# First blocks of the mixture of experts in plain fp32 for four experts, without split parts, and the table of places by one VectorE pass

## The chip, the cores and the metric

The kernel runs on one core of a Trainium2 chip. The metric is the device time of one execution in microseconds (us), lower is better. The times shown are a median of three runs; the profile is of one further execution.

## The reference

A windowed attention (8 batches, 8 heads, 576 tokens, head size 64, window 128) is followed by a mixture of experts with two experts chosen per token:

```python
scores = scale * q @ k^T + bias, masked to 0 <= i - j < 128
attn = softmax(scores); x = (attn @ v) as [4608, 512]
logits = x @ w_gate; noisy = logits + log1p(exp(x @ w_noise)) * noise
top2 = the two largest of noisy; top2_w = softmax over the two
for e in range(8):
    h = maximum(x[mask] @ w1[e], 0.0)          # 512 -> 1024
    out[mask] += top2_w * (h @ w2[e])          # 1024 -> 512
```

## The kernel before

The program is straight-line code whose order is made while it is built: strands of work (generators) yield operations with an engine, an estimated cost and a rank, a small planner (class Order) takes for each free engine the ready operation of lowest rank, and so writes every engine's queue. On the chip each queue runs in that order; a row whose input is late holds all rows behind it on its engine.

There are two phases. In the first, 96 attention units (4 pairs of heads times 3 groups of query blocks for each of 8 batches) are computed in fp32: scores (L455, L448), maxima and bias on VectorE (L473), exponentials on ScalarE (L480), transposes (L492) and the product with v (L523). When a batch is done, its rows are transposed and stored (L632, L635), and `route` computes the gates, ranks the tokens of each expert by a small matmul (L723 to L727), and builds two tables: `which_line` (L759) and `which_place` (L765, ten instructions of 64 columns per batch), whose product on TensorE (L770) lists token numbers per expert. GpSimd scatters that list to memory (L843). Batch b + 1 is routed only when batch b is.

After two batches, NF = 5 experts each have at least FIRST = 256 listed tokens (places are padded up to that), and TensorE fills gaps of the attention with these first blocks: 5 blocks of 256 tokens, each in 8 steps of 128 hidden units. A step is an up product into one PSUM bank (`ups`, `mm1`, L1086), a relu (`middle`, L1108 or L1110), and a down product into two banks (`downs`, `mm2`, L1136). Operands are split into a high and a low part in fp32r, and each product is three matmuls (high by high, low by high, high by low). The parts cost other engines work: a weight tile is cast (ScalarE or VectorE) and subtracted (L962, GpSimd or VectorE), the tokens too (L1079), and the hidden units (L1125, VectorE).

In the second phase all other tokens are computed with f16 parts, three matmuls per product as well. Each expert has room for 1216 tokens: an expert with a first block has 960 left, in blocks of 512 and 448; the others have blocks of 512, 384 and 320 (`BLOCKS`). The last block of each expert but the last one is computed turned round (`mm2_flipped`, L1141). Tiles of the first phase end in a (axh, w1ha, ahh), those of the second begin with b or end in b (bxh, w1hb, bhh). The second phase can begin when batch 7 is listed and its tokens are gathered (L1034), scaled, turned and split.

The lines that name the sizes and the splits:

```python
CUTS = (2,)
FIRST = (256,)
NF = 5
BLOCKS = (((256, 512), (768, 448)), ((0, 512), (512, 384), (896, 320)))
second.extend(Block(e, s0, c, NPAD, rings2) for e in range(E) for s0, c in BLOCKS[e >= NF])
```

## Time and profile before

| what | value |
|---|---|
| median of 3 runs | 1215.79 us (1214.66 to 1219.39) |
| profiled execution | 1212.61 us |
| its span, first to last instruction | 1210.7 us |
| PE (TensorE) busy | 1142.3 us, 94% of the span |
| DVE (VectorE) busy | 775.9 us, 64% |
| ACT (ScalarE) busy | 547.3 us, 45% |
| POOL (GpSimd) busy | 310.7 us, 26% |
| mean granted TensorE clock | 0.988 of full |

Busy shares are means over stages that differ: the attention, a short stage in which the rest of the first blocks and the routing of the last batches are left, and the second phase. A matmul's duration in the trace holds its time through the array as well, so that TensorE can be counted busy while it starts nothing new; how dense it is worked is read from the starts of its instructions.

### The profile page before, as it was taken

The numbers are of one execution on the slowest core, as the hardware profiler recorded it, in microseconds if no ns is written. First come the engines' busy times: TensorE is split into PE (matmuls) and PEld (weight loads), VectorE is DVE, ScalarE is ACT, GpSimd is POOL, SyncE is SP. The second block draws the span as 40 slices with busy tenths as digits, with TensorE's granted clock in tenths as the row PEclk, the third lists the DMA queues.
The fourth block names the chain that finished last, engine by engine and source line by source line (L and its number), as shares of the span: only waits on it lengthen the run. The fifth ranks groups of instructions, "written<-read, shape, count | busy, mean of one in ns | idle before, by whom it ended". The sixth has DMA issues, their size and how long they took to land.

```text
span 1210.7 us, 20898 instructions
## 1 busy us (share of the span) xinstructions
PE 1142.3 (94%) x7336; PEld 690.1 (57%) x7336; DVE 775.9 (64%) x2483; ACT 547.3 (45%) x1378; POOL 310.7 (26%) x343
## 2 busy tenths in 40 slices
PE   7998899999997889999999999999999999999995
PEld 4666677777776764554544544545545654575552
DVE  6798787788898897664664674584563473373310
ACT  8776666667633353441432433342432441252311
POOL 5000121231255661320330331233033320332211
PEclk9999999999999999999999999999999999999998
DMA  8896545553267597562761862663663391352221
GB/s 289 281 319 208 172 130 172 161 151 125 77 184 179 125 280 217 134 186 91 178 187 45 206 171 54 186 191 58 193 166 62 80 264 41 62 114 45 35 27 23
DMA packets 138987, 177.57 MB, mean 147 GB/s; under 512 B 25728, under 2 KB 89472, under 8 KB 138880
## 3 DMA queue, kind: packets, MB, share of 16 engines
q1 hardware_dynamic: 120960, 135.87, 35.3%
q0 software_dynamic: 17920, 40.33, 17.5%
q8 instruction: 59, 0.97, 0.3%
q14 instruction: 48, 0.39, 0.1%
HBM read 134.76 MB, written 41.40 MB: 146 GB/s over the span
## 4 chain that ended last, share of the span: by engine, by line
PE 58%; DVE 13%; DMA 8%; issue 4%; POOL 1%; ACT 0%; SPq 0%; POOLq 0%; another core or an unknown queue 0%; DVEq 0%
PE bank L1086 23%; PE bank L1136 16%; PE bank L1141 8%; DMA mraw<-in_w_dram 5%; PE bank L523 2%; PE bank L492 2%; DMA xg<-xs_dram,ix 2%; DVE wam L988 2%; PE bank L1066 2%; PE bank L455 2%; DVE hot L765 1%; POOL out_dram L1215 1%; DVE bxl L1076 1%; DVE fit L1051 1%; DMA raw<-in_w_dram 1%
## 5 line engine op out<-in xcount | busy, mean ns | idle before, releaser
L1125 DVE SCALAR_TENSOR_TENSOR bhl<-bank,bhh 128x512 f16<-128x512 f32 (+3 forms) x152 | 93.9, 618 | 282.9 <-ACT bhh L1108 282.7
L1215 POOL DMA_INDIRECT out_dram<-yo,ix x70 | 110.3, 1575 | 534.3 <-ACT yo L245 480.4
L1108 ACT ACTIVATE bhh<-bank 128x512 f16<-128x512 f32 (+3 forms) x143 | 77.7, 543 | 332.8 <-PE bank L1086 331.9
L1086 PE MATMUL bank<-bxh,w1hb 128*128 128x512 f16 (+3 forms) x608 | 213.5, 351 | 0.0
L1086 PE MATMUL bank<-bxl,w1hb 128*128 128x512 f16 (+3 forms) x608 | 213.4, 351 | 0.0
L1086 PE MATMUL bank<-bxh,w1lb 128*128 128x512 f16 (+3 forms) x608 | 213.4, 351 | 0.0
L1086 PEld LDWEIGHTS <-w1hb 128*128 128x128 f16 x1216 | 118.0, 98 | 104.8 <-issue 1.9
L480 ACT ACTIVATE p<-p,nm 128x256 f32<-128x256 f32 (+2 forms) x288 | 133.8, 469 | 8.5 <-DVE nm L473 8.4
L1136 PE MATMUL bank<-w2hb,bhl 128*128 128x512 f16 (+1 forms) x352 | 133.5, 379 | 4.2 <-DVE bhl L1125 4.2
L1136 PE MATMUL bank<-w2hb,bhh 128*128 128x512 f16 (+1 forms) x352 | 133.7, 380 | 0.6 <-ACT bhh L1108 0.5
L1136 PE MATMUL bank<-w2lb,bhh 128*128 128x512 f16 (+1 forms) x352 | 133.4, 379 | 0.0
L1136 PEld LDWEIGHTS <-bhh 128*128 128x128 f16 (+1 forms) x704 | 67.3, 98 | 72.9 <-issue 4.6
L473 DVE CUSTOM_DVE_ANT_0 p<-bank,bias 128x256 f32<-128x256 f32 (+2 forms) x288 | 95.5, 380 | 17.4 <-PE bank L455 15.8
L1086 PEld LDWEIGHTS <-w1lb 128*128 128x128 f16 x608 | 59.5, 98 | 54.7
L962 POOL TENSOR_TENSOR w1la<-raw,w1ha 128x512 fp32r<-128x512 f32 x35 | 48.7, 1392 | 161.9 <-ACT w1ha L245 115.2
L523 PE MATMUL bank<-pT,vraw 128*64 128x128 f32 (+3 forms) x896 | 81.2, 303 | 5.6 <-ACT p L480 3.3
L492 PE MATMUL bank<-ident,p 128*128 128x128 f32 x512 | 83.2, 287 | 1.6 <-DVE pT L249 0.7
L1034 POOL DMA_INDIRECT xg<-xs_dram,ix x70 | 70.0, 1000 | 43.0 <-issue 37.9
L988 DVE TENSOR_REDUCE wam<-mraw 128x1 f32<-128x1024 f32 x56 | 67.7, 1211 | 19.9 <-DMA mraw<-in_w_dram 19.6
L455 PE MATMUL bank<-qk 64*128 64x256 f32 (+1 forms) x512 | 70.7, 389 | 10.2 <-DVE nm L473 5.3
L1141 PE MATMUL bank<-bhl,w2hb 128*128 128x448 f16 (+1 forms) x224 | 75.5, 337 | 0.0
L1141 PE MATMUL bank<-bhh,w2lb 128*128 128x448 f16 (+1 forms) x224 | 75.5, 337 | 0.0
(219 smaller groups left out, 2119.9 us busy)
## 6 DMA issues: line engine op xcount, KB each, us to landing
raw<-in_w_dram SPq DMA_DIRECT2D x208, 256.0 KB, 3.9
mraw<-in_w_dram SPq DMA_DIRECT2D x56, 512.0 KB, 6.6
qk<-in_qk_dram SPq DMA_DIRECT2D x32, 608.0 KB, 4.5
out_dram<-xg SPq DMA_DIRECT2D x10, 1024.0 KB, 8.6
vraw<-in_v_dram SPq DMA_DIRECT2D x16, 512.0 KB, 3.9
xs_dram<-x SPq DMA_DIRECT2D x32, 256.0 KB, 3.4
vraw<-in_v_dram SPq DMA_DIRECT2D x16, 128.0 KB, 5.5
xg<-xs_dram,ix POOLq DMA_INDIRECT x70, 4.8
```

The lines of the kernel that those rows point to most:

```text
L455: nc.tensor.matmul(s[h][:, o:o + c], qk[half, i * 128:i * 128 + 128], qk[half, QW + k0:QW + k0 + c], start=True, stop=True)
L473: nc.vector.tensor_tensor_reduce(out=p[:, z, h, 0:c], in0=s[h][:, o:o + c], in1=bv, scale=-0.125, scalar=3.0e38, op0=OP.add, op1=OP.min, a ...
L480: nc.scalar.activation(pv, pv, AF.Exp, bias=nm[:, z, h:h + 1], scale=-1.0, accum_out=den[:, z, 2 * g + h:2 * g + h + 1])
L492: nc.tensor.transpose(t[:, z], p[:, h, a:a + 128], ident)
L523: nc.tensor.matmul(o[half, o0:o0 + c], t[p0:128, kb, hh:hh + D], w, start=m == 0, stop=m == len(lst) - 1)
L988: yield dve(1.13, rank, lambda: nc.vector.tensor_reduce(o, t, axis=AX.X, op=OP.max, apply_absolute_value=True))
L1086: nc.tensor.matmul(t[:, 0:blk.n], wp[:, c], x[:, c, 0:blk.n], start=c == 0 and z == 0, stop=c == 3 and z == 2)
L1108: nc.scalar.activation(o, i, AF.Relu)
L1125: yield dve(0.07 + c * 0.00104, rank - MIDDLE, lambda: nc.vector.scalar_tensor_tensor(hl[:, 0:c], t[:, 0:c], 0.0, high, op0=OP.max, op1=OP ...
L1136: nc.tensor.matmul(blk.y[j][0:r], h[:, cs], wp, start=f == 0 and m == 0, stop=f == 7 and m == 2)
L1141: nc.tensor.matmul(blk.y[c][:, 0:blk.n], wp[:, c * 128:c * 128 + 128], h[:, 0:blk.n], start=f == 0 and m == 0, stop=f == 7 and m == 2)
L1215: ins = nc.gpsimd.indirect_dma_start(out=out, out_offset=bass.IndirectOffsetOnAxis(ap=blk.ix[0:r, j:j + 1], axis=0), in_=t[0:r], in_offset ...
```

## The change

Four experts instead of five have a first block, and these blocks are computed in plain fp32: one matmul per product, no cast, no subtraction, no low parts. A weight tile is loaded straight into its set, of which there are 8 instead of 5, and the ring of hidden tiles has 3 instead of 2. Expert 4 goes over to the other row of BLOCKS: 512, 384 and 320 tokens in the second phase instead of 512 and 448. The planner's costs of the first steps change with them (up `blk.n / 600` per row chunk, down 0.86). The table of places is made by one VectorE instruction of 640 columns with 0 and 1, and five ScalarE instructions multiply the token numbers in, beside `which_line`. GpSimd keeps its DMAs and a few fills.

```diff
-NF = 5
+NF = 4
...
-        def which_place(i):
-
-            for k in range(2):
-                V.tensor_scalar(hot[1][:, 2 * i + k], steps_[:, 0:LINE], d[:, i, k:k + 1], numbers[:, i:i + 1],
-                                op0=OP.is_equal, op1=OP.mult)
+        def which_place():
+
+            shape = [128, 2 * NQ, LINE]
+            V.tensor_tensor(hot[1], d.rearrange("p i k -> p (i k)")[:, :, None].to_broadcast(shape),
+                            steps_[:, None, 0:LINE].to_broadcast(shape), op=OP.is_equal)
+
+        def numbered(i):
+
+            nc.scalar.activation(hot[1][:, 2 * i:2 * i + 2], hot[1][:, 2 * i:2 * i + 2], AF.Copy, scale=numbers[:, i:i + 1])
...
+        yield dve(0.81, rank, which_place)
+        numbering = [act(0.3, rank, lambda i=i: numbered(i), False) for i in range(NQ)]
+        for op in numbering[:-1]:
+            yield op
+        end = yield numbering[-1]
         yield dve(0.98, rank, which_line)
-        for i in range(NQ):
-            yield dve(0.28, rank, lambda: which_place(i))
+        yield end
...
-    wsets = [Ring([weight_set(keep, F32R, f"a{z}") for z in range(5)]), Ring([])]
+    wsets = [Ring([(keep.tile([128, 4, 128], F32, name=f"w1a{z}"), keep.tile([128, DM], F32, name=f"w2a{z}"))
+                   for z in range(8)]), Ring([])]
...
-    rings1 = block_rings(keep, FIRST[0], F32R, "a", 2)
+    rings1 = block_rings(keep, FIRST[0], F32, "a", 3)
...
-    def weight(t, r, hi, lo, ev, rank, src, e, z, f):
+    def weight(t, ev, rank, src, e, z, f):
         yield from move(2.6e5, rank, lambda: nc.sync.dma_start(t, src))
-        yield either(0.52, 0.34, rank, LATE[5], lambda g: copy(g, hi, t))
-        yield Op((("POOL", 1.23, rank), ("DVE", 0.6, rank + WEIGHTS_LATE)),
-                 lambda g: engine[g].tensor_sub(lo, t, hi.bitcast(F32)))
-        put(r, t)
         mark(ev)
...
     def mm1(blk, t, w, cc):
         for c in cc:
+            if blk not in second:
+                nc.tensor.matmul(t[:, 0:blk.n], w[0][:, c], blk.xh[:, c, 0:blk.n], start=c == 0, stop=c == 3)
+                continue
...
-            us = 3 * (blk.n / 2400 + (0.005 if p else 0.016))
+            us = 3 * (blk.n / 2400 + 0.005) if p else blk.n / 600
...
-        yield dve(0.07 + c * 0.00104, rank - MIDDLE, lambda: nc.vector.scalar_tensor_tensor(
-            hl[:, 0:c], t[:, 0:c], 0.0, high, op0=OP.max, op1=OP.subtract))
+        if blk in second:
+            yield dve(0.07 + c * 0.00104, rank - MIDDLE, lambda: nc.vector.scalar_tensor_tensor(
+                hl[:, 0:c], t[:, 0:c], 0.0, hh[:, 0:c], op0=OP.max, op1=OP.subtract))
...
     def mm2(blk, f, j, r, w):
         cs = slice(j * 128, j * 128 + r)
+        if blk not in second:
+            nc.tensor.matmul(blk.y[j][0:r], blk.h[f][1][0][:, cs], w[1], start=f == 0, stop=f == 7)
+            return
```

How the rows move. On TensorE, where the attention's last products with v stand (L523 before, L522 after; pT holds the turned weights, w1a and w2a the first blocks' weights), the program before has:

```order
L523 MATMUL bank_72<-pT_91,vraw_82 64x128 x4
L655 MATMUL bank_69<-xu_95,wgn 32x256 x4
L1086 MATMUL bank_71<-axh_208,w1ha_174 128x256
L1086 MATMUL bank_71<-axl_210,w1ha_174 128x256
L1086 MATMUL bank_71<-axh_208,w1la_175 128x256
L435 MATMUL bank_73<-diag,one 128x2
L523 MATMUL bank_72<-pT_92,vraw_82 64x64 x4
```

At the same place on TensorE the changed program has:

```order
L1147 MATMUL bank_72<-w2a_183,ahh_205 128x512
L522 MATMUL bank_70<-pT_91,vraw_82 64x256 x2
L522 MATMUL bank_70<-pT_91,vraw_82 64x128 x4
L631 MATMUL bank_73<-ident,xu_95 128x128 x4
L631 MATMUL bank_69<-ident,xu_95 128x128 x4
L1093 MATMUL bank_71<-axh_204,w1a_184 128x256 x2
```

Ahead of the last L523, 16 up products and 15 down products of first blocks stand before, so 24 and 25 are behind it; ahead of the last L522, 13 and 13 stand after the change, so 19 and 19 are behind it. Of these 19, 10.5 stand ahead of the last list matmul of batch 7 (L773) and 8.5 between it and the first row of the second phase; before, 15 stood ahead of that list and 9 behind it (up products).

On VectorE, where the last batch's tables are made (hot_167 is the table of lines, hot_168 that of places; ahl is a low part of hidden units, w1la and w2la are of weights), the program before has:

```order
L962 TENSOR_TENSOR w1la_179<-raw_116,w1ha_178 128x512
L759 TENSOR_TENSOR hot_167<-ef,steps 128x800
L765 TENSOR_SCALAR hot_168<-steps,d,numbers 128x64 x4
L1125 SCALAR_TENSOR_TENSOR ahl_214<-bank_67,ahh_212 128x256
L765 TENSOR_SCALAR hot_168<-steps,d,numbers 128x64 x4
L962 TENSOR_TENSOR w2la_185<-raw_120,w2ha_184 128x512
L765 TENSOR_SCALAR hot_168<-steps,d,numbers 128x64 x2
L1125 SCALAR_TENSOR_TENSOR ahl_213<-bank_71,ahh_211 128x256
L962 TENSOR_TENSOR w2la_189<-raw_118,w2ha_188 128x512
L777 TENSOR_SCALAR listed<-bank_73 80x64
```

At the same place on VectorE the changed program has:

```order
L741 CAST d<-si 128x10
L764 TENSOR_TENSOR hot_168<-d,steps 128x640
L1120 TENSOR_SCALAR ahh_206<-bank_71 128x256
L758 TENSOR_TENSOR hot_167<-ef,steps 128x800
L780 TENSOR_SCALAR listed<-bank_73 80x64
```

Ten instructions have become one, the five subtractions of first blocks between them are gone, and one relu stands there; five ScalarE rows (L769) now lie between L764 and the list matmul.

## Rows read from the trace of the kernel before

**Rows 1.** Stretch; busy us of PE, PEld, DVE, ACT, POOL; granted clock, DMA share, GB/s.

```profile
140.00:340.00 200.00, 194.02 (x1710) 143.36 (x1707) 165.79 (x732) 135.04 (x466) 46.34 (x42) 1.00 0.44 135
340.00:444.00 104.00, 86.68 (x590) 73.51 (x589) 93.21 (x253) 41.27 (x90) 59.95 (x56) 0.95 0.69 186
```

**Rows 2.** TensorE in order of time (start, us): where stages and experts begin.

```profile
336.99 0.60 PE L523 MATMUL bank<-pT,vraw 128*64 128x64 f32 x8
...
444.28 0.39 PE L1086 MATMUL bank<-bxh,w1hb 128*128 128x512 f16 x1
...
526.88 0.38 PE L1086 MATMUL bank<-bxh,w1hb 128*128 128x512 f16 x1
...
871.00 0.38 PE L1086 MATMUL bank<-bxh,w1hb 128*128 128x512 f16 x1
...
1090.02 0.38 PE L1086 MATMUL bank<-bxh,w1hb 128*128 128x512 f16 x1
```

**Rows 3.** Groups on TensorE, 337 to 444: count | busy us, mean ns | idle ahead, releaser.

```profile
L1136 PE MATMUL bank<-w2ha,ahl 128*128 128x512 f32 x49 | 21.4, 436 | 13.5 <-DVE ahl L1125 13.3 <-DVE ix L885 0.2
...
L1066 PE MATMUL bank<-ident,xg 128*128 128x128 f32 x32 | 5.0, 278 | 1.1 <-DMA xg<-xs_dram,cl 1.0
L632 PE MATMUL bank<-ident,xu 128*128 128x128 f32 x24 | 3.7, 276 | 0.0
L770 PE MATMUL bank<-hot,hot 128*80 128x64 f16 x30 | 2.6, 199 | 2.6 <-DVE hot L765 2.6
```

**Rows 4.** Groups on VectorE, 340 to 444.

```profile
L1125 DVE SCALAR_TENSOR_TENSOR ahl<-bank,ahh 128x256 fp32r<-128x256 f32 x24 | 9.9, 414 | 5.6 <-ACT ahh L1108 5.6
L765 DVE TENSOR_SCALAR hot<-steps,d,numbers 128x64 f16<-128x64 f16 x20 | 9.5, 533 | 0.0
L962 DVE TENSOR_TENSOR w2la<-raw,w2ha 128x512 fp32r<-128x512 f32 x9 | 7.5, 828 | 1.1 <-ACT w2ha L245 1.1
```

**Rows 5.** Chain that ended last, 337 to 444: shares by line, longest pieces (start, us).

```profile
by line: DMA xg<-xs_dram,ix 10.0%; DVE hot L765 7.7%; DMA raw<-in_w_dram 7.1%; PE bank L1136 7.0%; DVE l L789 5.8%; DMA mraw<-in_w_dram 5.7%; issue 5.6%; DVE ahl L1125 4.8%; DVE bias L1298 4.6%; PE bank L1086 3.0%; DVE x L635 2.8%; DVE w2la
...
410.06 4.88 DVE bias L1298
```

**Rows 6.** VectorE, then GpSimd, in order of time around 381 to 387.

```profile
381.09 0.20 DVE L788 TENSOR_TENSOR l<-l,noi 128x40 f32<-128x40 f32 x1
381.32 6.16 DVE L789 TENSOR_TENSOR l<-l,lg 128x40 f32<-128x40 f32 x1
...
381.85 1.88 POOL L962 TENSOR_TENSOR w2la<-raw,w2ha 128x512 fp32r<-128x512 f32 x1
...
385.58 1.83 POOL L962 TENSOR_TENSOR w1la<-raw,w1ha 128x512 fp32r<-128x512 f32 x1
```

**Rows 7.** TensorE in order of time: first-block matmuls, up and down.

```profile
406.41 0.28 PE L1086 MATMUL bank<-axh,w1ha 128*128 128x256 f32 x1
406.52 0.27 PE L1086 MATMUL bank<-axl,w1ha 128*128 128x256 f32 x1
...
443.14 0.40 PE L1136 MATMUL bank<-w2la,ahh 128*128 128x512 f32 x1
443.37 0.39 PE L1136 MATMUL bank<-w2ha,ahl 128*128 128x512 f32 x1
```

**Rows 8.** TensorE in order of time: one fp32 matmul of 192 columns, two records.

```profile
62.56 0.49 PE L448 MATMUL bank<-qk 128*128 128x192 f32 x2
62.89 0.28 PE L492 MATMUL bank<-ident,p 128*128 128x128 f32 x1
```

**Rows 9.** One line each: duration ns min/median/max of tables, and of fp32 weight loads.

```profile
L765 DVE TENSOR_SCALAR hot<-steps,d,numbers x80: 207/293/1321, 87.2 to 407.8; 128x64 f16<-128x64 f16 x80
...
L759 DVE TENSOR_TENSOR hot<-ef,steps x8: 979/985/1094, 86.3 to 402.2; 128x800 f16<-128x800 f32 x8
...
L448 PEld LDWEIGHTS bank<-qk x64: 186/190/332, 11.0 to 324.8; 128*128 128x128 f32 x64
```

**Rows 10.** Groups by shape, whole span: a ScalarE copy.

```profile
L245 ACT ACTIVATE xu<-bank 128x256 f32<-128x256 f32 x35 | 13.4, 382 | 25.2 <-PE bank L523 23.2 <-DVE wam L966 1.6
```

More of the change, by code (lines that the diff above doesn't have):

```diff
@@ L9 @@
 F32 = mybir.dt.float32
-F32R = mybir.dt.float32r
 F16 = mybir.dt.float16
@@ L898, in block_rings @@
     def block_rings(pool_, c, dt, name, hn):
-        return {"xh": ring(pool_, 2, [128, 4, c], dt, name + "xh"), "xl": ring(pool_, 2, [128, 4, c], dt, name + "xl"),
-                "hh": ring(pool_, hn, [128, c], dt, name + "hh"), "hl": ring(pool_, hn, [128, c], dt, name + "hl")}
-    wsets = [Ring([weight_set(keep, F32R, f"a{z}") for z in range(5)]), Ring([])]
+        return {r: ring(pool_, 2 if r[0] == "x" else hn, [128, 4, c] if r[0] == "x" else [128, c], dt, name + r)
+                for r in (("xh", "hh") if dt == F32 else ("xh", "xl", "hh", "hl"))}
+    wsets = [Ring([(keep.tile([128, 4, 128], F32, name=f"w1a{z}"), keep.tile([128, DM], F32, name=f"w2a{z}"))
+                   for z in range(8)]), Ring([])]
     wam = keep.tile([128, 2, 2, 8], F32, name="wam")
@@ L940, in weights @@
                 ev = chunks[p, e, f] = [Event(), Event(), None]
+                if p == 0:
+                    w = ev[2] = yield (wsets[p], r)
+                    mark(named[p, e, f])
+                    for z, src in enumerate((first_weight(e, f), second_weight(e, f))):
+                        spawn(weight(w[z], ev[z], r + 0.2 * z, src, e, z, f))
+                    continue
                 a = yield (raw1, r)
@@ L946, in weights @@
                 for z, (t, rg, src) in enumerate(((a, raw1, first_weight(e, f)), (b, raw2, second_weight(e, f)))):
-                    make = weight if p == 0 else scaled_weight
-                    spawn(make(t, rg, w[2 * z], w[2 * z + 1], ev[z], r + 0.2 * z, src, e, z, f))
+                    spawn(scaled_weight(t, rg, w[2 * z], w[2 * z + 1], ev[z], r + 0.2 * z, src, e, z, f))
     def first_weight(e, f):
@@ L1030, in tokens @@
         blk.xh = yield (blk.rings["xh"], rank)
-        blk.xl = yield (blk.rings["xl"], rank)
+        if blk in second:
+            blk.xl = yield (blk.rings["xl"], rank)
         for j, r in blk.tiles:
@@ L1072, in turn_tokens @@
         mark(blk.weighed)
-        hi, lo = blk.xh[:, :, cs], blk.xl[:, :, cs]
+        hi = blk.xh[:, :, cs]
+        yield either(0.48, 0.6, rank, LATE[6], lambda e: copy(e, hi, tv))
         if blk in second:
-            yield either(0.48, 0.6, rank, LATE[6], lambda e: copy(e, hi, tv))
-            yield dve(0.6, rank, lambda: nc.vector.tensor_sub(lo, tv, hi))
-        else:
-            yield either(0.48, 0.6, rank, LATE[6], lambda e: copy(e, hi, tv))
-            yield dve(0.6, rank, lambda: nc.vector.tensor_sub(lo, tv, hi.bitcast(F32)))
+            yield dve(0.6, rank, lambda: nc.vector.tensor_sub(blk.xl[:, :, cs], tv, hi))
         put(tb, a)
@@ L1084, in mm1 @@
         for c in cc:
+            if blk not in second:
+                nc.tensor.matmul(t[:, 0:blk.n], w[0][:, c], blk.xh[:, c, 0:blk.n], start=c == 0, stop=c == 3)
+                continue
             for z, (wp, x) in enumerate(((w[0], blk.xh), (w[0], blk.xl), (w[1], blk.xh))):
@@ L1116, in middle @@
             put(blk.rings["xh"], blk.xh)
-            put(blk.rings["xl"], blk.xl)
+            if blk in second:
+                put(blk.rings["xl"], blk.xl)
         hh = yield (blk.rings["hh"], rank)
         blk.h[f][1].append(hh)
-        hl = yield (blk.rings["hl"], rank)
-        blk.h[f][1].append(hl)
+        if blk in second:
+            hl = yield (blk.rings["hl"], rank)
+            blk.h[f][1].append(hl)
         yield either(0.052 + c * 0.000833, 0.067 + c * 0.00104, rank - MIDDLE, LATE[8], lambda e: relu(
             e, hh[:, 0:c], t[:, 0:c]))
-        high = hh[:, 0:c] if blk in second else hh[:, 0:c].bitcast(F32)
-        yield dve(0.07 + c * 0.00104, rank - MIDDLE, lambda: nc.vector.scalar_tensor_tensor(
-            hl[:, 0:c], t[:, 0:c], 0.0, high, op0=OP.max, op1=OP.subtract))
+        if blk in second:
+            yield dve(0.07 + c * 0.00104, rank - MIDDLE, lambda: nc.vector.scalar_tensor_tensor(
+                hl[:, 0:c], t[:, 0:c], 0.0, hh[:, 0:c], op0=OP.max, op1=OP.subtract))
         put(hbr, t)
@@ L1165, in downs @@
             for j, r in blk.tiles:
-                end = yield pe(0.655 if p else 0.69, rank, lambda: mm2(blk, f, j, r, ev[2]), False)
+                end = yield pe(0.655 if p else 0.86, rank, lambda: mm2(blk, f, j, r, ev[2]), False)
                 if f == 7:
```

3 lines of the change are left out of this document (1 added, 2 removed).

## The prediction

> **What bounds the kernel now.** I read the table of stretches first, then where stages begin on TensorE, then in the middle stage the waits, the groups and the chain.
>
> While attention runs together with first blocks, TensorE is busy 194.0 of 200 us [rows 1]. The last product of the attention starts at 336.99, the first matmul of the second phase at 444.28 [rows 2]. These 107.3 us hold the rest of the first blocks and the routing of batches 6 and 7, and here TensorE is not the limit: 86.7 busy of 104 at a mean granted clock of 0.95, beside VectorE with 93.2 [rows 1]. TensorE's largest named wait is 13.5 us ahead of the third matmul of a down product, for the low part of the hidden units, and the list matmuls wait 2.6 for the table of places [rows 3]. The chain through this stage is mostly VectorE and what VectorE lets go late: the table of places 7.7%, low parts 4.8%, a weight load 7.1%, and two tiny instructions (L789 5.8%, L1298 4.6%, one of them 4.88 us long) [rows 5].
>
> The second phase starts expert 1 at 526.88, expert 5 at 871.00, expert 7 at 1090.02 [rows 2]. Experts 1 to 4, with two blocks, thus take (871.00 - 526.88) / 4 = 86.0 us each, experts 5 and 6, with three, (1090.02 - 871.00) / 2 = 109.5.
>
> **Price of a step on TensorE.** Before, matmuls of an up product start 0.11 to 0.12 us apart (I take 0.115), those of a down product 0.23 [rows 7]: a step of 12 and 6 takes 1.38 + 1.38 = 2.76. After, it has 4 fp32 matmuls of 256 columns and 2 of 512. The one fp32 shape that fills the array's rows and columns has 192 columns and is followed by the next instruction after 0.33 us [rows 8], 1.72 ns per column, so 0.44 and 0.88, and the step 4 x 0.44 + 2 x 0.88 = 3.52. The first blocks as a whole stay what they were: 40 x 2.76 = 110 before, 32 x 3.52 = 113 after. The change gives TensorE nothing here; it takes waiting away, and it adds work to the second phase.
>
> **Until the attention ends.** By the order, 16 up and 15 down products stood ahead of its last product, 16 x 1.38 + 15 x 1.38 = 42.8 us; now 13 of each, 45.8: +3.0. Against that, ScalarE and VectorE lose casts of weights at the start, where both also work for the first attention units (-1.5, two or three casts of 512 columns at 0.6, if 256 take 0.38 [rows 10]), and in the mixed part a short VectorE instruction no longer waits for GpSimd (-3). TensorE's 6 us of counted idle time there [rows 1] bound the last from above. Sum -1.5, between -6 and +3.
>
> **The middle stage.** Before: 24 up and 25 down products, 67.6 us, and other TensorE work of about 11 (the three largest groups are busy 11.3 [rows 3], counted with their time in the array, and small ones come on top). Of 107.3 us, 28.7 are lost. After: 19 x 3.52 = 66.9, the same 11, and what is still lost. VectorE loses in this stretch 24 low parts (9.9), the ten-piece tables (9.5), nine subtractions of second weights (7.5) [rows 4] and smaller ones; it gains two instructions of 640 columns, at 985 / 800 ns per column [rows 9] 0.8 each. So some 30 of 93 us go, and a down product waits for one relu alone. What stays is routing: between a batch's ranks and its list stand two steps of first blocks, 7 us, against a chain of some fifteen short VectorE instructions (3 us at L788's 0.20 [rows 6]), the pass of 0.8 and five ScalarE copies. Their 128 columns have no row; they cost between nothing seen and the 0.38 of 256 columns [rows 10], I take 0.3, 1.5 together, of which 1.0 lies beside the table of lines [rows 9]. I take 5 us of loss in all, between 0 and 12. Stage: 66.9 + 11 + 5 = 82.9, that is -24.4, between -29 and -17.
>
> The weight loads cost nothing: a set is free of casts and eight are in flight, which covers 8 x 3.5 = 28 us. If that cover failed, a wait like the 7.1% of the chain [rows 5], 7.6 us, would come back. The ScalarE copies hide behind ScalarE's idle time, 41.3 busy of 104 [rows 1].
>
> **The second phase.** Expert 4 gets a third block: 109.5 - 86.0 = +23.5. I allow 1.5 either way, since blocks differ in how well their turns are covered.
>
> **Sum.** 1212.6 (the profiled execution, 3.2 below the median of the runs) - 1.5 - 24.4 + 23.5 = 1210.2. I forecast 1210, for the median too, since the extra of 3.2 is within what those three runs differ by. Its own range, from the ends above, is 1203 to 1217. About 0.5% is what a measurement of this kernel can tell from no change: 1210 is 0.5% under the median, at the border.
>
> **Short waits that come with GpSimd.** L789 works on 40 columns, as L788 does in 0.20 us, yet took 6.16, and ended when four GpSimd subtractions in a row, from 381.85 to 387.41, ended [rows 6]. L765 takes 0.21 alone and up to 1.32 [rows 9]. These rows alone don't say whether GpSimd's remaining DMA instructions would hold VectorE as well; the forecast takes it that they don't. The Trainium skill, SBUF — State Buffer, section "SBUF: two separate sides", says that a VectorE instruction with two inputs in SBUF is blocked for a whole instruction only by a GpSimd one that reads SBUF too, and one in a two-port mode by any that holds the pair; by that, L789's 6.0 us of waiting must go and the sum is as above; L1298, of another kind, could still wait for a GpSimd DMA instruction, and the sum would be about 5 higher at most.
>
> **Rivals.**
> - **The lists come late, and the time rises.** TensorE's order is fixed: batch 7's list stands behind 10.5 steps, and the second phase 8.5 further on. If list or gathered tokens are later than that, everything stands. The chain before needed the whole 107 us. Of it the change surely takes the low parts (5.1) and some 5 of the 8.2 for the table of places. The weight load (7.6), L789 (6.0) and L1298 (4.7) [rows 5, 6] go only if loads come early and bursts alone made the waits. If they stay, the stage gives back 12 instead of 24.4: 1212.6 - 1.5 - 12 + 23.5 = 1222.6. It decides below 22 us given back. For it: VectorE was the fuller engine. Against: with all of it gone, 28 and the subtractions of some 3 more, the chain ends at 444 - 31 = 413, ahead of TensorE's work (337 - 1.5 + 82.9 = 418).
> - **More than that is given back.** The attention itself may have been held by VectorE and GpSimd, in gaps too short to count as idle, since a matmul's time in the array covers them. If the mixed part runs 3% shorter, 6 us, and the middle stage loses 1 instead of 5, the time is 1210 - 6 - 4 = 1200. Against: only 6 of 200 us are idle there.
> - **Weight loads bind the fp32 matmuls.** Two loads of 0.19 us belong to each (64 records for 32 matmuls [rows 9]). If they were not covered, a step would take 6 x 2 x 0.19 = 2.3 more and 32 steps 73: 1283. Against: the pair of records with its loads takes 0.33 for 192 columns [rows 8], so they are covered already there, and 256 and 512 columns cover more. The Trainium skill, TensorE: Matmul & The Clock Gate, section "Weight-path perf modes — Fast Weight Load (FWL) and DoubleRow", says that fp32 weights get no fast load, which speaks against the change; where a load is covered it alters nothing.
>
> **How the numbers follow.** The forecast's case (1203 to 1217) gets 0.55, the late lists (1217 to 1228) 0.25, more given back (1196 to 1203) 0.17, bound weight loads 0.03. Of the first, half lies below 1209.7 (0.5% under the median): with the third that is 0.42 faster, after a little is taken off for a third case that stops short. Slower, over 1221.9, is half of the late lists and the loads, 0.16; 0.42 is left for no change. 1198 to 1222 holds the first case, most of the third and the nearer part of the second, 8 in 10.
>
> **What would show it.** Right: the second phase starts at about 418 (415 to 425); first-block down products no longer wait; VectorE is at some 60% in the middle stage and no 40-column instruction takes microseconds; up matmuls of first blocks are about 0.44 apart; expert 4 takes 109 to 110 us. Wrong: long TensorE waits at the list matmuls or at the second phase's first turns (late lists); fp32 matmuls further apart than 0.45 (loads); the attention's last product well ahead of 330 (more given back); or an expert 4 that costs much less than 23 more.

## The result and the profile after

The changed kernel takes 1197.95 us (median of 4 runs, 1196.58 to 1198.55), the kernel before 1215.22 (4 runs, 1214.08 to 1219.39): a ratio of 0.9865 (0.9842 to 0.9889), 17 us less. That is 12 below the forecast of 1210, below the range of its own case (1203 to 1217), at the very end of the wide range (1198 to 1222), and about the time of the rival "more than that is given back" (1200). The profiled execution took 1197.38 us, its span is 1195.5.

The stages first: TensorE's rows in order of time, which answer to [rows 2].

```profile
322.27 1.09 PE L522 MATMUL bank<-pT,vraw 128*64 128x256 f32 x12
...
405.58 0.38 PE L1096 MATMUL bank<-bxh,w1hb 128*128 128x512 f16 x1
...
492.52 0.38 PE L1096 MATMUL bank<-bxh,w1hb 128*128 128x512 f16 x1
...
749.75 0.38 PE L1096 MATMUL bank<-bxh,w1hb 128*128 128x512 f16 x1
...
859.05 0.38 PE L1096 MATMUL bank<-bxh,w1hb 128*128 128x512 f16 x1
...
1075.35 0.38 PE L1096 MATMUL bank<-bxh,w1hb 128*128 128x512 f16 x1
```

The last matmul of the attention's last group starts at 323.1 (337.4 before), and the stages below are counted from there. The second phase starts at 405.58 instead of 444.28. The rows from 405.58 on are the starts of experts 0, 1, 4, 5 and 7.

| stage | before | after | change | predicted |
|---|---|---|---|---|
| to the start of the attention's last matmul | 337.4 | 323.1 | -14.3 | -1.5 |
| from there to the second phase | 106.9 | 82.5 | -24.4 | -24.4 |
| second phase, to the last matmul's start | 753.2 | 777.2 | +24.0 | +23.5 |

Inside the second phase expert 4 takes 109.3 us instead of 85.5, +23.8; expert 0 takes 86.9 instead of 82.6, and what the others do adds up to -4. Two of the three terms are met within half a microsecond, the first is not.

The table of stretches, with the columns of [rows 1], over the mixed part and over the middle stage:

```profile
140.00:340.00 200.00, 200.00 (x1632) 133.01 (x1629) 149.13 (x704) 124.08 (x444) 13.25 (x16) 1.00 0.47 139
...
340.00:418.00 78.00, 73.69 (x334) 46.31 (x333) 51.13 (x175) 32.93 (x67) 21.15 (x24) 0.98 0.75 209
```

In the middle stage TensorE is now busy 94% (before 83%), VectorE 66% (before 90%). GpSimd has 13.25 us of work in the mixed part instead of 46.34. By the clock records of the two traces, the granted clock is at its lower level (1.2 of 2.4 GHz) for 3.4 us of the middle stage instead of 10.2. Before, behind the longest wait for a low part (5.12 us, to 390.29), it fell, and nine down matmuls in a row started 0.43 us apart instead of 0.23: part of what the waits cost is that clock.

Groups on TensorE in the middle stage, 323 to 406, with the columns of [rows 3], and behind them single rows in order of time:

```profile
L1147 PE MATMUL bank<-w2a,ahh 128*128 128x512 f32 x72 | 37.0, 627 | 3.6 <-DVE fit L439 3.6
L1093 PE MATMUL bank<-axh,w1a 128*128 128x256 f32 x152 | 36.8, 380 | 0.0
...
L773 PE MATMUL bank<-hot,hot 128*80 128x64 f16 x30 | 1.6, 202 | 0.0
```

```profile
353.89 1.89 PE L1093 MATMUL bank<-axh,w1a 128*128 128x256 f32 x8
355.61 1.88 PE L1147 MATMUL bank<-w2a,ahh 128*128 128x512 f32 x4
357.33 1.03 PE L1093 MATMUL bank<-axh,w1a 128*128 128x256 f32 x4
```

The 13.5 us ahead of the down products and the 2.6 ahead of the list [rows 3] are gone; 3.6 are left, at one place. A step is 1.72 + 1.72 = 3.44 us (3.52 predicted): eight records of 256 columns, two to a matmul, are 0.43 per up matmul, four of 512 are 0.86 per down matmul.

Some instructions of the routing one line at a time: duration min/median/max in ns, and first and last start in us. They answer to L789, L1298 and L765 in [rows 5, 6, 9].

```profile
L792 DVE TENSOR_TENSOR l<-l,lg x8: 189/196/200, 67.9 to 357.7; 128x40 f32<-128x40 f32 x8
...
L1313 DVE TENSOR_SCALAR bias<-bias x1: 174/174/174, 368.7 to 368.7; 1x8 int32<-1x8 int32 x1
...
L764 DVE TENSOR_TENSOR hot<-d,steps x8: 761/822/826, 82.0 to 364.0; 128x640 f16<-128x640 f32 x8
...
L769 ACT ACTIVATE hot<-hot,numbers x40: 384/386/402, 82.9 to 366.0; 128x128 f16<-128x128 f16 x40
```

The short instructions are short in every batch: the one that took 6.16 us takes 0.20, the one of 4.88 takes 0.17. If I add up over all VectorE instructions ahead of the second phase what each takes above the usual duration of its own line and shape, I get 34 us before and 0.5 after (L1298 and L1313, which stand once, are not in it). The 0.5 after are two instructions that began during a DMA instruction of GpSimd, of 101 that did, about 0.25 us each; L1313, beside another, was not held. So GpSimd's remaining DMA instructions hold VectorE hardly at all, as the forecast took it. A numbering copy takes 0.386 us, where 0.3 was taken.

### The profile page after: what moved, and what is told of

It is laid out like the page before. It is cut to its first block, busy times and chain, and to the rows that moved or that the text cites. A ratio compares the mean times of both kernels' runs of the same rounds, so it can differ in the third digit from the quotient of the medians.

```text
span 1195.5 us, 20195 instructions
## 1 busy us (share of the span) xinstructions
PE 1150.3 (96%) x7164; PEld 667.7 (56%) x7164; DVE 706.7 (59%) x2356; ACT 526.8 (44%) x1351; POOL 224.6 (19%) x280
## 4 chain that ended last, share of the span: by engine, by line
PE 79%; DVE 8%; DMA 7%; issue 4%; ACT 1%; POOL 1%; SPq 1%; POOLq 0%; another core or an unknown queue 0%; DVEq 0%; ACTq 0%
PE bank L1096 24%; PE bank L1151 17%; PE bank L1156 7%; PE bank L522 6%; PE bank L491 5%; PE bank L454 5%; DMA mraw<-in_w_dram 4%; PE bank L1093 4%; PE bank L1147 4%; PE bank L1076 2%; DVE wam L997 2%; PE bank L631 2%; PE bank L654 1%; DMA raw<-in_w_dram 1%; PE bank L447 1%
## 5 line engine op out<-in xcount | busy, mean ns | idle before, releaser
L1096 PE MATMUL bank<-bxh,w1hb 128*128 128x512 f16 (+3 forms) x640 | 223.0, 348 | 0.0
L1096 PE MATMUL bank<-bxl,w1hb 128*128 128x512 f16 (+3 forms) x640 | 222.8, 348 | 0.0
L1096 PE MATMUL bank<-bxh,w1lb 128*128 128x512 f16 (+3 forms) x640 | 222.6, 348 | 0.0
L1096 PEld LDWEIGHTS <-w1hb 128*128 128x128 f16 x1280 | 124.8, 98 | 107.3 <-issue 3.5
L1151 PE MATMUL bank<-w2hb,bhl 128*128 128x512 f16 (+1 forms) x376 | 142.6, 379 | 3.6 <-DVE bhl L1137 3.6
L1151 PE MATMUL bank<-w2hb,bhh 128*128 128x512 f16 (+1 forms) x376 | 142.8, 380 | 0.5 <-ACT bhh L1118 0.5
L1151 PE MATMUL bank<-w2lb,bhh 128*128 128x512 f16 (+1 forms) x376 | 142.5, 379 | 0.0
L1151 PEld LDWEIGHTS <-bhh 128*128 128x128 f16 (+1 forms) x752 | 72.0, 98 | 78.1 <-issue 4.6
L522 PE MATMUL bank<-pT,vraw 128*64 128x128 f32 (+3 forms) x896 | 81.7, 305 | 1.6 <-ACT pT L244 0.7
L522 PEld LDWEIGHTS bank<-pT,vraw 128*64 128x64 f32 (+1 forms) x896 | 51.3, 136 | 41.6 <-issue 8.5
L1156 PE MATMUL bank<-bhh,w2hb 128*128 128x448 f16 (+1 forms) x224 | 73.8, 330 | 0.0
```

The source lines that it names most:

```text
L522: nc.tensor.matmul(o[half, o0:o0 + c], t[p0:128, kb, hh:hh + D], w, start=m == 0, stop=m == len(lst) - 1)
L1096: nc.tensor.matmul(t[:, 0:blk.n], wp[:, c], x[:, c, 0:blk.n], start=c == 0 and z == 0, stop=c == 3 and z == 2)
L1151: nc.tensor.matmul(blk.y[j][0:r], h[:, cs], wp, start=f == 0 and m == 0, stop=f == 7 and m == 2)
L1156: nc.tensor.matmul(blk.y[c][:, 0:blk.n], wp[:, c * 128:c * 128 + 128], h[:, 0:blk.n], start=f == 0 and m == 0, stop=f == 7 and m == 2)
```

## The experiments

The question is which part of the change gives the two gains, in the attention and in the middle stage. The theories: GpSimd's subtractions hold VectorE's short instructions (the routing); the load of parts on ScalarE and VectorE makes the attention late; the ten-piece table does; the low part of the hidden units makes the down products wait; deeper rings cover loads.

All runs in one table. Ratios are to the kernel before on the same chip (the experiments ran on three chips, so the ratios are to be compared and not the medians). "Last product", "last list" (L770 or its like) and "second phase" are starts from each profile's TensorE rows. The last two columns are my own sums over each trace: the time from each matmul's start to the next one's, up to the attention's last product, for matmuls of first blocks (with the up and down products that they make) and for all others. They and the starts come from one profiled execution of each kernel.

| kernel | median | ratio (95%) | last product | last list | second phase | first blocks | others |
|---|---|---|---|---|---|---|---|
| before | 1215.22 | 1 | 337.4 | 408.1 | 444.3 | 56.1 (16, 15) | 276.5 |
| after | 1197.95 | 0.9865 (0.9842 to 0.9889) | 323.1 | 367.7 | 405.6 | 49.0 (13, 13) | 269.5 |
| t1_table_only | 1209.77 | 0.9974 (0.9956 to 0.9992) | 328.2 | 399.5 | 436.4 | 52.5 (15, 15) | 271.1 |
| n4_split | 1222.18 | 1.0087 (1.0053 to 1.0121) | 329.5 | 395.5 | 429.7 | 48.2 (13, 13) | 276.7 |
| v1_no_gpsimd | 1198.01 | 0.9883 (0.9857 to 0.9909) | 339.0 | 392.7 | 426.7 | 60.0 (17, 16.5) | 274.3 |
| t2_old_table | 1194.63 | 0.9870 (0.9839 to 0.9901) | 322.1 | 367.7 | 402.2 | 49.2 (13, 13) | 268.3 |
| g1_gpsimd_reads | 1207.87 | 0.9963 (0.9942 to 0.9983) | 323.8 | 374.3 | 413.6 | 50.6 (13, 13) | 268.3 |
| g2_gpsimd_writes | 1206.87 | 0.9939 (0.9916 to 0.9962) | 326.1 | 376.2 | 415.4 | 49.0 (13, 13) | 272.2 |
| n5_plain | 1200.57 | 0.9899 (0.9870 to 0.9927) | 330.6 | 378.8 | 435.8 | 58.7 (16, 15) | 267.1 |
| r1_shallow | 1193.05 | 0.9831 (0.9787 to 0.9874) | 322.7 | 366.2 | 404.0 | 51.5 (13.75, 13) | 266.5 |
| h1_low_part | 1195.23 | 0.9861 (0.9817 to 0.9904) | 327.0 | 370.4 | 404.8 | 52.0 (14, 13) | 270.2 |
| c1_casts | 1202.57 | 0.9913 (0.9889 to 0.9938) | 329.9 | 378.0 | 414.5 | 52.7 (14, 13.5) | 272.7 |
| c2_all_parts | 1206.38 | 0.9945 (0.9922 to 0.9969) | 332.5 | 382.1 | 420.0 | 54.3 (14, 13) | 273.6 |
| b1_shallow_old_table | 1194.86 | 0.9855 (0.9831 to 0.9880) | 321.5 | 368.2 | 402.2 | 49.2 (13, 13) | 267.7 |

The first four kernels take the change apart.

**t1_table_only** is the kernel before with the table of the change.

```diff
-            for k in range(2):
-                V.tensor_scalar(hot[1][:, 2 * i + k], steps_[:, 0:LINE], d[:, i, k:k + 1], numbers[:, i:i + 1],
+            V.tensor_tensor(hot[1], d.rearrange("p i k -> p (i k)")[:, :, None].to_broadcast(shape),
...
+        yield dve(0.81, rank, which_place)
+        numbering = [act(0.3, rank, lambda i=i: numbered(i), False) for i in range(NQ)]
```

> The kernel before with the new table of places alone (one VectorE pass, numbers by ScalarE); five experts, split parts and GpSimd subtractions stay. Theory A (VectorE's load): in the trace of before the ten-piece tables cost VectorE 20.4 us in six batches, the pass costs 4.8 in the kernel after, so attention ends some 5 to 8 us ahead of 337 and the time is about 1206 to 1210. Theory B (GpSimd's bursts hold VectorE): the subtractions are still there, so the pass and its neighbours still wait, 2 to 4 us gained, 1211 to 1213. Theory C (the planner's order, by chance): no relation, within 3 us of 1215.

Measured: 0.26% less, 1212 if the ratio is applied to 1215.22, the time of theory B. The attention ends 9.2 us earlier, as theory A had it and more; 3.6 of them are in the first-block matmuls, of which one up product fewer stands ahead of its end. The middle stage stays at 108 us (328.2 to 436.4), so the table is not what the routing waited for, though the chain before named it with 7.7% [rows 5].

**t2_old_table** is the kernel after with the ten-piece table.

```diff
-            V.tensor_tensor(hot[1], d.rearrange("p i k -> p (i k)")[:, :, None].to_broadcast(shape),
...
+            for k in range(2):
+                V.tensor_scalar(hot[1][:, 2 * i + k], steps_[:, 0:LINE], d[:, i, k:k + 1], numbers[:, i:i + 1],
```

> The kernel after with the ten-piece table put back; four experts, plain fp32, no GpSimd subtraction. Theory A: attention ends 5 to 8 us later than 323 and the time is about 1204 to 1206. Theory B: alone, without bursts, a piece costs 0.21 to 0.29 us, so 3 us at most are lost, 1199 to 1201. Theory C: 1195 to 1201 with no shift that goes with VectorE's busy time.

Measured: 0.987 beside 0.9865, no loss. With no parts to make, the ten pieces cost nothing; the theory that VectorE's work for the table held the kernel falls for the kernel after.

**n4_split** is the kernel before with four first blocks in split parts.

```diff
-NF = 5
+NF = 4
```

> The kernel before with four experts with a first block instead of five; split parts, GpSimd and the ten-piece table stay. The second phase gets 23.5 us longer, as predicted for expert 4. The first gives back 8 steps: at TensorE's 2.76 us each 22 us (TensorE-bound: 1215 + 1.5 = 1217), at what a step took in the middle stage of before, 107 us for 24, 4.3 to 4.5 us each, 35 us (VectorE-bound: 1204). Theory of the prediction: nearer the second, 1204 to 1210; a rival, that routing alone sets the middle stage's end: it gives back nothing, 1235.

Measured: 0.9% slower, 1226 by the ratio, between the TensorE-bound 1217 and the 1235 of the rival; the theory of the prediction (1204 to 1210) fails. Fewer blocks alone cost the third block of expert 4 and get back only 14.6 us at the start of the second phase (444.3 to 429.7). The waits of TensorE from 320 to 445 (what waits, for whom; total us, count, longest):

```profile
PE bank L1136 <- DVE ahl L1125: 9.2, 7, 2.7
PE bank L1066 <- DVE fit L440: 5.2, 1, 5.2
```

The down products still wait for low parts, and the second phase for its tokens. This run gives a second thing that I had not asked it for, by its columns on the right: its 13 and 13 products cost 48.2 us among the attention, about as much as the 13 and 13 plain ones of the kernel after (49.0).

**g1_gpsimd_reads** is the kernel after, with a subtraction on GpSimd for each of the 64 first weight tiles into a spare tile that nobody reads.

```diff
+    def idle_part(t, z, rank):
+        yield pool(1.23, rank, lambda: nc.gpsimd.tensor_sub(spare_part[z], t, t))
...
+        spawn(idle_part(t, z, rank))
```

> The kernel after plus one GpSimd subtraction per first weight tile (64 in all) that reads the tile and writes a spare tile nobody reads; left in are one pass for the table, plain fp32, four experts. Theory B: short VectorE instructions last microseconds again where these stand in a row, attention ends 5 or more us later, the time is 1205 to 1212. Theory A (only VectorE's and ScalarE's own work counted): within 2 us of 1198. Theory C: within 4 us of 1198, no stretched VectorE instructions.

Measured: 1.0% of the kernel's time comes back, though nothing waits for these subtractions. In order of time, VectorE and then GpSimd of g1_gpsimd_reads, and one line of VectorE by itself:

```profile
355.62 6.16 DVE L751 TENSOR_TENSOR tmp<-mine,line 80x8 f32<-80x8 f32 x1
...
356.24 1.54 POOL L975 TENSOR_TENSOR sp<-w1a 128x512 f32<-128x512 f32 x1
...
360.55 1.19 POOL L975 TENSOR_TENSOR sp<-w1a 128x512 f32<-128x512 f32 x1
```

```profile
L751 DVE TENSOR_TENSOR tmp<-mine,line x7: 154/157/6155, 90.5 to 355.6; 80x8 f32<-80x8 f32 x7
```

An instruction of 8 columns that takes 0.157 us took 6.155, and it ends at 361.78, when the last subtraction of the burst ends (361.74). It is the picture of [rows 6], made to order. The last product of the attention hardly moves (323.1 to 323.8), the last list moves by 6.6 and the second phase by 8.0: GpSimd's price lies in the routing, not in the attention, where theory B had put it; its time (1205 to 1212) is met. A rival is that GpSimd itself, with subtractions in its queue, came late to its own work on the lists. The traces speak against it: ahead of the scatter of the last list GpSimd had sat idle, for 3.19 us in the kernel before, 0.45 here and 4.20 in g2_gpsimd_writes.

**g2_gpsimd_writes** puts a fill that reads nothing in place of each subtraction.

```diff
+    spare_part = keep.tile([128, 1280], F32, name="sp")
...
+        yield pool(1.23, rank, lambda: nc.gpsimd.memset(spare_part, 0.0))
```

> The kernel after plus one GpSimd fill of 1280 columns per first weight tile (64, about as long as a subtraction) that reads nothing. If it is the reading of SBUF by GpSimd that holds VectorE instructions with two inputs in SBUF (the Trainium skill, SBUF — State Buffer, section SBUF: two separate sides, says so), none of these is stretched and the time is within 3 us of 1198, against 1208 with subtractions. If any GpSimd instruction of that length holds VectorE, it is 1204 to 1210 and the stretched instructions are back.

Measured: 0.9939, so the fills cost about as much as the subtractions; I had expected next to nothing. Single lines of g2_gpsimd_writes, as above:

```profile
L792 DVE TENSOR_TENSOR l<-l,lg x8: 189/196/201, 68.1 to 366.2; 128x40 f32<-128x40 f32 x8
...
L804 DVE TENSOR_SCALAR d<-d x8: 157/166/1416, 75.8 to 369.4; 128x5 f32<-128x5 f32 x8
...
L975 POOL MEMSET sp<- x64: 1165/1166/1772, 3.9 to 387.6; 128x1280 f32 x64
```

It is other instructions that are held. Of 235 TENSOR_TENSOR ahead of 460 us none is stretched; 11 TENSOR_SCALAR beside a GpSimd instruction are, by 10.8 us in all, and 5 casts, by 4.5. One SCALAR_TENSOR_TENSOR with two inputs is longer by 1.4 (L892 at 384.86); it stands behind a held TENSOR_SCALAR (L1336, 384.24, 2.17 us) and ends with it. In g1_gpsimd_reads it is 12 TENSOR_TENSOR by 14.0 and 8 TENSOR_SCALAR by 4.5 (my own count over the trace, above the shortest of the same line and shape; lines that stand once are not in it). Of the TENSOR_TENSOR with two inputs in SBUF that begin while a subtraction is under way, all 10 are stretched in g1_gpsimd_reads and all 11 in the kernel before; of those that begin during a fill, none of 17 in g2_gpsimd_writes. The Trainium skill, SBUF — State Buffer, section "SBUF: two separate sides", says this: an instruction with two inputs in SBUF is held for a whole GpSimd instruction that reads SBUF, one in a two-port mode for any GpSimd instruction. The trace agrees on the first half by these counts. On the second it agrees in that one-input instructions are held by fills as well; which of them ran in a two-port mode the profile doesn't show. My expectation had used the first half alone. The hold can last longer than the one instruction: L751 in g1_gpsimd_reads was held over five.

**v1_no_gpsimd** is the kernel before with the subtractions of first weights on VectorE alone, all else kept: five blocks, split parts, ten-piece table.

```diff
-        yield Op((("POOL", 1.23, rank), ("DVE", 0.6, rank + WEIGHTS_LATE)),
-                 lambda g: engine[g].tensor_sub(lo, t, hi.bitcast(F32)))
+        yield dve(0.6, rank + WEIGHTS_LATE, lambda: nc.vector.tensor_sub(lo, t, hi.bitcast(F32)))
```

> The kernel before with all subtractions of weights on VectorE (17 before, 80 here) and none on GpSimd; five experts, split parts, old table. Theory B: the stretched VectorE instructions are gone (34 us in the first phase before), against 63 x 0.7 = 44 us more VectorE work, so within 5 us of before, 1208 to 1218. If bursts cost nothing but what VectorE's own load hides, it is slower by 10 or more, 1223 and up.

Measured: 0.9883, nearly all that the whole change brings, where I had expected a small part. Of v1_no_gpsimd the stretch from 339 to 427 (columns of [rows 1]), then two lines of VectorE:

```profile
339.00:427.00 88.00, 81.98 (x587) 68.86 (x584) 78.53 (x264) 41.69 (x90) 22.93 (x24) 0.98 0.68 189
```

```profile
L789 DVE TENSOR_TENSOR l<-l,lg x8: 187/199/203, 68.3 to 380.0; 128x40 f32<-128x40 f32 x8
...
L765 DVE TENSOR_SCALAR hot<-steps,d,numbers x80: 210/296/354, 82.2 to 392.1; 128x64 f16<-128x64 f16 x80
```

The middle stage is 87.7 us instead of 106.9, with the low parts, the ten pieces and all subtractions on VectorE, whose busy share stays at 89% (78.53 of 88). L789 no longer takes 6 us, a piece of the table at most 0.354 instead of 1.321 [rows 9]. TensorE's waits for the low part of the hidden units from 320 to 445 (total us, count, longest), 13.3 in the kernel before [rows 3] and 10.6 in t1_table_only, are all but gone:

```profile
PE bank L1135 <- DVE ahl L1124: 0.3, 1, 0.3
```

That a subtraction takes less time on VectorE than on GpSimd is not what helped: in this stretch of the kernel before TensorE waited for no low part of a weight. VectorE was not too full in the middle stage; it was held.

**n5_plain** is the kernel after with five first blocks.

```diff
-NF = 4
+NF = 5
```

> The kernel after with five experts with a first block, plain fp32. The second phase gets 23.5 us shorter. The first gets 8 steps of 3.45 us, 27.6: if TensorE bounds it, 1198 + 4 = 1202; if it has room left before the second phase's tokens are ready (3.6 us of waiting there), 1198; more if weight loads or banks run short, 1206.

Measured: 0.9899, 0.3% behind the kernel after, as expected where TensorE bounds it (1202), though the two intervals overlap. It is also the same as v1_no_gpsimd (0.9883) within the intervals: at five blocks, plain products with no parts at all are worth no more than the parts taken off GpSimd.

The next three ask which load of the parts makes the attention late.

**h1_low_part** is the kernel after with a low part of every first hidden tile made into a spare tile, for which the down product waits.

```diff
+        if blk not in second:
+            yield dve(0.07 + c * 0.00104, rank - MIDDLE, lambda: nc.vector.scalar_tensor_tensor(
+                spare_low[f % 2][:, 0:c], t[:, 0:c], 0.0, hh[:, 0:c], op0=OP.max, op1=OP.subtract))
```

> The kernel after plus the VectorE low part of the hidden units in each first step (32 of 0.41 us), written to a spare tile; the bank and the down product wait for it as before. Theory of the prediction (down products waited 13.5 us for it): the middle stage gets 3 to 8 us longer, 1201 to 1206. Rival, that these waits came from VectorE being full of other work: the extra 0.4 us per step is covered by the other two banks, within 2 us of 1198.

Measured: 0.9861, no cost, and a middle stage of 78 us. The 13.5 us that TensorE waited for the low parts before [rows 3] are thus not their price: as v1_no_gpsimd shows with the split products themselves, they came late because VectorE was held.

**c1_casts** is the kernel after with the cast of every first weight tile into a spare tile, on ScalarE or VectorE, waited for.

```diff
+        yield either(0.52, 0.34, rank, LATE[5], lambda g: copy(g, spare_hi[z][f % 4], t))
```

> The kernel after plus one copy of each first weight tile (64, on ScalarE or VectorE as the planner chose the casts before) into a spare tile, which the products wait for. Theory L (ScalarE's and VectorE's work on weights is what was given back beside GpSimd's 10 us): attention ends 4 to 10 us later than 323, the time is 1203 to 1210. Rival (the casts were covered): within 3 us of 1198.

**c2_all_parts** is c1_casts with the subtractions (GpSimd or VectorE, as the planner takes them) and the low parts as well, all into spare tiles.

```diff
+        yield either(0.52, 0.34, rank, LATE[5], lambda g: copy(g, spare_hi[z][f % 4], t))
+        yield Op((("POOL", 1.23, rank), ("DVE", 0.6, rank + WEIGHTS_LATE)),
+                 lambda g: engine[g].tensor_sub(spare_lo[z], t, spare_hi[z][f % 4]))
```

> The kernel after with the parts' work put back around plain fp32 products: copies of weight tiles, subtractions on GpSimd or VectorE, low parts of hidden units, all into spare tiles, waited for as before (the token tiles' low parts stay out). If this work is what made the first phase of the split kernel with four experts last to 430 us, the second phase starts here at 425 to 440 and the time is 1216 to 1230, although the products are the same as in the kernel after. Rival, that the split products themselves (three matmuls, their loads and banks) made it: 1208, as with GpSimd's subtractions alone.

Measured: the casts give back 0.5% of the time (theory L), all parts together 0.8%, about the 1208 of the second run's rival and not the 1216 to 1230 of its theory. Of the 24.1 us by which n4_split starts its second phase later than the kernel after, all parts make 14.4, and GpSimd's subtractions alone 8.0 (g1_gpsimd_reads); the other 9.7 lie with the split products, the token tiles' low parts or the order, which no run tells apart. In the column of the other matmuls the casts add 3.2 us to the 269.5 of the kernel after and all parts 4.1, of 7.0 between the kernels. That would be somewhat over half of the difference, but kernels without any added load differ by 3.0 in this column, so it is a hint and not a measurement.

**r1_shallow** is the kernel after with the ring depths of before, **b1_shallow_old_table** has the ten-piece table too.

```diff
-                   for z in range(8)]), Ring([])]
+                   for z in range(5)]), Ring([])]
...
-    rings1 = block_rings(keep, FIRST[0], F32, "a", 3)
+    rings1 = block_rings(keep, FIRST[0], F32, "a", 2)
```

> The kernel after with five first weight sets instead of eight and two hidden tiles instead of three. Theory of the prediction: eight sets cover 28 us, five 17 us, both more than a load takes, and the hidden ring is emptied step by step: within 3 us of 1198. Rival, that the depth is what the change gives: the wait for a weight load is back, up to 8 us, 1203 to 1208.

> The kernel after with the ten-piece table and the shallow rings (five weight sets, two hidden tiles): the two versions that came out level or a little lower, together. Theory: both parts change nothing by themselves and the 3 to 5 us between them are the planner's order: 1193 to 1200. If the two gains are real and add: 1188 to 1192.

Measured: 0.9831 and 0.9855, about 1195 and 1198 by the ratio, near what was expected, and intervals that overlap with the kernel after. Eight sets and three hidden tiles bring nothing over five and two, and no version here is measurably ahead of the change.

## Why the forecast was off, step by step

**Price of a step.** Right where it was read. Steps in a row take 3.44 us after (3.52 predicted), and before 0.115 and 0.23 apart [rows 7].

**Until the attention ends: the step that failed.** It was put at -1.5 and measured -14.3. Its first part, 16 up and 15 down products against 13 and 13, was put at 42.8 to 45.8, +3.0; by the table it went from 56.1 to 49.0, -7.1. Its second part, what ScalarE and VectorE lose, was put at -4.5 and is -7.0. The forecast's own sign for this case, a last product well ahead of 330, is there; the second phase, awaited at about 418, starts at 405.6.

The error in the first part is that [rows 7] lie in the middle stage, where products of first blocks follow each other, and the price read there was used for the mixed part, where they come singly between attention matmuls. TensorE's rows of the kernel before in the mixed part, in order of time (start, us):

```profile
208.33 0.60 PE L492 MATMUL bank<-ident,p 128*128 128x128 f32 x4
208.68 0.36 PE L1086 MATMUL bank<-axh,w1ha 128*128 128x256 f32 x1
208.88 0.28 PE L1086 MATMUL bank<-axl,w1ha 128*128 128x256 f32 x1
209.00 0.29 PE L1086 MATMUL bank<-axh,w1la 128*128 128x256 f32 x1
209.22 1.14 PE L455 MATMUL bank<-qk 64*128 64x256 f32 x8
```

From 208.68 to 209.22 are 0.54 us for three matmuls that take 0.35 in a row. The first needs 0.20 to the next start instead of 0.12: it comes behind an fp32 matmul, and is itself of split parts in fp32r (behind an f16 or bf16 matmul it needs 0.08 more as well). The last needs 0.22: behind it comes another shape of the array (64*128 instead of 128*128). Over the mixed part, all 66 entries into a piece of split parts take 0.08 to 0.14 us above a matmul inside a piece, also where the shape of the array stays. The kernel after at about the same place:

```profile
200.86 1.88 PE L1147 MATMUL bank<-w2a,ahh 128*128 128x512 f32 x4
202.58 0.60 PE L491 MATMUL bank<-ident,p 128*128 128x128 f32 x4
...
204.17 0.66 PE L491 MATMUL bank<-ident,p 128*128 128x128 f32 x4
204.66 1.46 PE L1093 MATMUL bank<-axh,w1a 128*128 128x256 f32 x6
206.06 1.09 PE L522 MATMUL bank<-pT,vraw 128*64 128x256 f32 x12
```

Four down records between two groups of the same shape take 1.72, as in a row. Six up records take 1.40, 0.467 per matmul: three times 0.43 and 0.1 for the change to 128*64 behind them; the entry, behind fp32 of the same shape, costs nothing. So in the mixed part a split step costs 29.9 / 16 + 26.2 / 15 = 3.62 us and a plain one 24.9 / 13 + 24.1 / 13 = 3.77, where the prediction had 2.76 and 3.52. n4_split shows it at equal counts: 48.2 split, 49.0 plain, 0.8 apart where the prediction's prices make it 9.9 (2.0 of the 48.2, and 1.9 of the 56.1, are time in which TensorE waited). What is left of the -7.1 is that fewer products stand ahead of the end. The Trainium skill, TensorEngine Tiling (Array Packing), section "Key Properties", says that a change of tiling mode drains TensorE. The 0.09 to 0.10 us between first-block matmuls and those of the scores (64*128), the gate (128*32) and the product with v (128*64) agree with it. Not every other shape costs that: behind first-block matmuls the list matmuls (128*80) and the transposes of 64 columns (128*64 too) begin without delay. The change from fp32 to split parts shows in the rows at one shape.

The second part, 7.0 us, is counted waiting: added up over the same matmuls, TensorE's counted idle time falls from 16.7 to 9.1 us, and without it the other matmuls take 259.8 before and 260.4 after. With the idle time among first-block matmuls it is 18.6 and 9.1, and of these 6.0 and 0.0 lie behind 140 us. Which load made TensorE wait is put in place less well. Added up at equal counts of score matmuls, 4.3 of the 7.0 are there when the third batch starts, 6.1 when the fifth does, ahead of nearly all first-block products. Casts return 3.2, all parts 4.1; t1_table_only takes 5.4 away while the parts are still made, and t2_old_table shows that the table is worth nothing without them. Such loads don't add up one by one, and kernels with plain products and no added load differ among themselves by 3.0 (266.5 to 269.5); whether by the planner's order or from one execution to the next, one profile of each doesn't tell. GpSimd's part in it is small: its subtractions add nothing to the kernel after (268.3), its fills 2.7 (272.2), and taking them off the kernel before saves 2.2 (274.3).

**The argument against the rival** that more comes back was that TensorE had only 6 of 200 us idle in the mixed part [rows 1]. As a bound on what counted waiting could give back there it held: all 6.0 were given back, where the forecast took 3. It does not bound the price of the pieces: the first matmul of a piece is counted busy for 0.36 instead of 0.28, so that its delay stands in busy time. The rival had the time about right (1200), but for other reasons in part: the waits that it called too short to count were counted, the price of the pieces it did not have, and its middle stage, with 4 us less of loss than forecast, did not come.

**The middle stage.** The size was right, -24.4; that it agrees to the tenth is luck, as the 5 us of loss in it were put between 0 and 12. That TensorE's own work bounds the stage once the waits are gone was right too. The reason why they go was half right. I made up the sum from what VectorE loses, 30 of 93 us, and from a down product that waits for one relu alone. v1_no_gpsimd keeps all of that work and still takes 19.2 us off the stage; h1_low_part puts the low parts back at no cost; t1_table_only removes the table's pieces and changes nothing there. What counted was the part that I had told as a side of it, that GpSimd's subtractions hold VectorE's short instructions: 34 us of stretched instructions before, 0.5 after, 1.3 in v1_no_gpsimd. The chain's shares for the table, the low parts and L789 [rows 5] were one cause under three names.

**Late lists.** Not met: the last list starts at 367.7 with no wait ahead of it. The rival's count, that some 10 us surely go with low parts and table, falls with the same runs.

**Weight loads** neither bind the fp32 matmuls (0.43 and 0.86 are the predicted pace) nor come late, with eight sets or with five.

**The copies on ScalarE** took 0.386 instead of 0.3, 0.4 us more for five, and no list matmul waits for them.

**The second phase.** Expert 4 costs 23.8 more (23.5 predicted). Expert 0 takes 4.3 longer, the largest wait at its start being 3.7 us for the low part of the tokens (L1086 of the kernel after), and the others regain about that.

**Sum.** 1212.6 - 14.3 - 24.4 + 24.0 = 1197.9, against 1197.4 profiled. The range of 1203 to 1217, said to come from the ends of the terms, is narrower than these ends added up (1200 to 1224); the time lies below both.

The gain can be put more simply by v1_no_gpsimd: with GpSimd out of the way the old products have 0.9883, and what the rest of the change adds to reach 0.9865 is within the intervals. The earlier second phase of the kernel after (405.6 instead of 426.7, 21 us) is paid out again by the third block of expert 4.

**Left open.** How the 7 us of waiting ahead of the attention's end divide among casts, subtractions and table; and whether the new table on top of v1_no_gpsimd would be ahead of the change, which was not run.

## What to carry to other kernels

Before work is spread over a third engine because it is idle, look for short VectorE instructions that take microseconds while GpSimd runs: one line's duration as min, median and max shows it, and the chain will blame whatever VectorE then does late. Price an instruction in the place where it will run: among what neighbours and after which kind of matmul, and read it from starts, since a delay inside the array counts as busy. An edit with several parts is worth one run with the smallest part alone; here one changed line brought most of the gain.

## What was not expected of the hardware

- A VectorE instruction can be held through a whole burst on GpSimd, not through a single instruction of it: 6.155 us for 8 columns, over five subtractions of 1.2 to 1.5 us (L751), and 6.16 over four of 1.8 to 1.9 (L789). Both, and L1298, began while a DMA instruction of GpSimd just ahead of the burst was under way. Others that began inside a subtraction ended with it although the next followed at once (L787 of g1_gpsimd_reads: 334.38 to 335.10, the subtraction to 335.04). Why is open.
- A GpSimd fill, which reads nothing, can hold VectorE's one-input instructions of 5 to 40 columns until it ends: 1.416 us instead of 0.166 for 5 columns.
- Going from an fp32 matmul to one in fp32r takes 0.08 us or more at the same array shape, and changing between 128*128 and the shapes of scores, gate and product with v 0.09; plain fp32 among fp32 has no such cost at its entry, but behind an f16 or bf16 matmul it has 0.08 too (0.299 instead of 0.216). Three fp32r matmuls that come singly among fp32 work are hardly cheaper than one fp32 matmul in two records: 0.47 us per chunk against 0.48 for 256 columns.
